# Token-major x and its logits: one 144-column product per 128 features, or a transposition and a 16-column product, on one Trainium2 core

## The chip, the core and the metric

The kernel runs on one core of a Trainium2 chip. The metric is device time in microseconds of one execution. Five engines work at the same time and wait for one another through semaphores: TensorE (PE, with its weight loads listed apart as PEld), VectorE (DVE), ScalarE (ACT), GpSimd (POOL) and SyncE (SP), which here only issues transfers. TensorE reads SBUF and writes PSUM; DVE and ACT take its results from there. A product on TensorE has two operands: one is loaded into the array first (lhsT, the weights), the other streams through it (rhs).

## What is computed

A retention layer feeds a mixture of experts that uses one expert for each token:

```python
scores = (q @ k.T) / 8 * Dmat            # 8 batches, 8 heads, 576 positions, 64 wide; Dmat[i,j] = gamma_h**(i-j) for i >= j
x = (scores @ v), as 4608 tokens x 512   # heads side by side
logits = x @ w_gate                      # 512 x 8
e = argmax(logits); gate = softmax(logits)[e]
eom = sigmoid(x @ w_output_gate)         # 512 x 8
out[token] = gate * eom[e] * relu(x @ w1[e]) @ w2[e]     # w1: 512 x 1024, w2: 1024 x 512, 8 experts
```

## The kernel before

The 4608 tokens are 36 tiles of 128. The work has two parts.

The first part is a loop over the tiles, `for g in range(NTILE)`, whose order is written out by hand under `tc.manual_schedule()`. In iteration g TensorE does, in this order: the scores of tile g+1 (`scores`, L361), the share of the running state in the output of tile g (`by_state`, L403), the share of the scores (`outT`, L412), the new state (`update`, L388), every fourth time a handful of small bf16 products for the slots of four tiles (`gate2`, L453 to L464), then k of tile g+1 turned to tokens (`k_rows`, L342) for some tiles, and last `xnat(g-1)` (L525). The state is reset every nine tiles (CPB), so `update` and `by_state` do nothing there. ACT copies state, k and x out of PSUM (L390, L344, L529) and casts expert weights; DVE masks the scores (L372), scales x (L416), and does the gate; POOL scales v (`prep`, L348) and scatters rows of x to a buffer in DRAM, sorted by expert (L191), with a small memset ahead of each scatter as a spacer.

`xnat` is what the change is about. `outT` leaves x of a tile as `xT`, 4 blocks of 128 features by 128 tokens. The experts want rows of x by tokens, and the gate wants 16 numbers a token (8 logits, 8 output gates). Both come from one product per block: lhsT is the block, rhs is `iw`, a constant of 144 columns that holds the identity (128 columns) and the 16 gate columns of that block side by side. In fp32 each product is two records in the trace, so a tile has 8 records, 4 into the bank `xa` and 4 into the bank `xb`. The gate columns lie so that in each bank the 16 columns of two blocks fall on the same place and add up. ACT then copies the tokens of each bank (two copies of 128x256), and DVE copies the 16 columns of `xa` and adds those of `xb` (L534, L535).

The state update needs k by tokens. It is loaded as features by tokens (in `pack`), and turned in one of two ways: by four transpositions against the identity on TensorE, 128x128 each and one record each, with a copy of 128x512 on ACT (`k_rows`); or by a second transfer of 256 KB from `krow`, a copy of k in DRAM by tokens (`load_k`). `by_rows(g)` says which: by transfer for odd g from 3 to 31. Tiles with g % 9 == 8 need none.

The second part, from 161 us on, is the experts: for each, h = x w1 and y = h w2 in products of fp32r with a high and a low part (L258, L279), weights streamed in by SP and split by ACT and DVE (L140, L145). Slots that got no token are filled by POOL scatters, with `G.memset(iw, 0.0)` ahead of each as a spacer (L709).

Of the kernel before, what the change touches and what calls it, by code (L numbers as in the profile page):

```python
# [10 lines left out]
F32 = mybir.dt.float32  # L11
# [4 lines left out]
ALU = mybir.AluOpType  # L16
# [7 lines left out]
DM = H * D  # L24
E = 8
F = 1024
P = 128
NP = H // 2
# [6 lines left out]
SNAP = 5  # L35
# [5 lines left out]
GT = 4  # L41
# [7 lines left out]
def tile_retention_moe(  # L49
# [17 lines left out]
    V, A, G, T, SP = nc.vector, nc.scalar, nc.gpsimd, nc.tensor, nc.sync  # L67

    const = ctx.enter_context(tc.tile_pool(name="const", bufs=1))
# [14 lines left out]
    ident = cmat_sb[:, 0, 0, :]  # L84
    gq_sb = const.tile([P, NP, 640], F32, name="gq_sb")
    gk_sb = const.tile([P, CPB, H, 1], F32, name="gk_sb")
    iw = const.tile([P, NP, 144], F32, name="iw")
    cbf_sb = const.tile([P, 2, P], BF16, name="cbf_sb")
    csm_sb = const.tile([P, 16 + 2 * CT], F32, name="csm_sb")
    base2 = const.tile([P, 1, E], F32, name="base2")  # L90
# [6 lines left out]
    xgrp = [const.tile([P, GT, XW], F32, name=f"xgrp{i}") for i in range(2)]  # L97
# [8 lines left out]
    def load_rest(step):  # L106
        if step < 3:
            n = slice(P * (step + 2), P * (step + 3))
            SP.dma_start(out=gq_sb[:, :, n], in_=gq[:, :, n])
        if step == 0:  # L110
            for p in range(NP):
                o = 0 if p % 2 == 0 else 16
                V.tensor_copy(iw[:, p, o:o + P], ident)
        elif step == 1:
            SP.dma_start(out=cmat_sb[:, 3], in_=cmat[:, 3])
        elif step == 2:
            SP.dma_start(out=cbf_sb, in_=cbf)
            SP.dma_start(out=csm_sb, in_=csm)
            SP.dma_start(out=tok_sb, in_=tokid)
            SP.dma_start(out=cov_sb, in_=cov)  # L120
            for x in xgrp:
                G.memset(x[:, :, DM:XW], 0.0)
            G.memset(zx.bitcast(I32)[:, DM:DM + 1], NT)
# [169 lines left out]
    ps_1 = p1ctx.enter_context(tc.tile_pool(name="ps_1", bufs=1, space=PSUM))  # L293
    ps_s = psctx.enter_context(tc.tile_pool(name="ps_s", bufs=1, space=PSUM, side="right"))

    pk, kn, vs, xT, gt = {}, {}, {}, {}, {}
# [10 lines left out]
    def load_first():  # L307
        t = [ld.tile([P, 3, 512], F32, name="pk") for _ in range(4)]
        pk.update(enumerate(t))
        SP.dma_start(out=t[0][:, 1], in_=pack[0, :, 1])  # L310
        A.dma_start(out=t[0][:, 0], in_=pack[0, :, 0])
        SP.dma_start(out=cmat_sb[:, 0:3], in_=cmat[:, 0:3])
        A.dma_start(out=t[0][:, 2], in_=pack[0, :, 2])
        SP.dma_start(out=gk_sb, in_=gk)
        A.dma_start(out=t[1][:, 0:2], in_=pack[1, :, 0:2])
        SP.dma_start(out=gq_sb[:, :, 0:P], in_=gq[:, :, 0:P])
        SP.dma_start(out=t[1][:, 2], in_=pack[1, :, 2])
        wgv = wg.rearrange("(p c) g -> c p g", c=P)
        SP.dma_start(out=iw[:, 0:NP:2, P:144], in_=wgv[:, 0:NP:2])
        SP.dma_start(out=iw[:, 1:NP:2, 0:16], in_=wgv[:, 1:NP:2])  # L320
        for i in (2, 3):
            if i == 3:
                SP.dma_start(out=gq_sb[:, :, P:2 * P], in_=gq[:, :, P:2 * P])
            SP.dma_start(out=t[i][:, 0:2], in_=pack[i, :, 0:2])
            SP.dma_start(out=t[i][:, 2], in_=pack[i, :, 2])

    def by_rows(g):
        return g % 2 == 1 and 1 < g < GT * SNAP + 12

    def load_k(g):  # L330

        if g < NTILE and g % CPB != 8 and by_rows(g):
            kn[g] = wk.tile([P, DM], F32, name="kn")
            SP.dma_start(out=kn[g], in_=krow[g])

    def k_rows(g):

        if g % CPB == 8 or by_rows(g):
            return
        ps = ps_s.tile([P, NP, P], F32, name="k_ps")  # L340
        for p in range(NP):
            T.transpose(ps[:, p, :], pk[g][:, 1, P * p:P * p + P], ident)  # L342
        kn[g] = wk.tile([P, DM], F32, name="kn")
        A.copy(out=kn[g], in_=ps.rearrange("p a i -> p (a i)"))  # L344
# [76 lines left out]
    def gate1a(n):  # L421
        L = gt["lg"]
        l, z = L[:, :, 0:8], L[:, :, 8:16]
        bc = lambda a: a.broadcast_to([P, GT, E])
        mx = sm.tile([P, GT, 1], F32, name="mx")
        V.tensor_reduce(out=mx, in_=l, op=ALU.max, axis=AX.X)
        lm = sm.tile([P, GT, E], F32, name="lm")
        V.tensor_tensor(out=lm, in0=l, in1=bc(mx), op=ALU.subtract)
        fst = sm.tile([P, GT, E], F32, name="fst")
        V.tensor_tensor(out=fst, in0=l, in1=bc(mx), op=ALU.is_equal)  # L430
        gt["half"] = (n, fst, lm, z)
# [85 lines left out]
            V.tensor_tensor(out=base2[:, 0, 0:1], in0=base2[:, 0, 0:1], in1=bump, op=ALU.add)  # L517

    def xnat(g):
        xa = ps_1.tile([P, 512], F32, name="xa")  # L520
        xb = ps_1.tile([P, 512], F32, name="xb")
        for p in range(NP):
            dst = xa if p < 2 else xb
            o = 0 if p % 2 == 0 else P
            i = T.matmul(dst[:, o:o + 144], lhsT=xT[g][:, p, :], rhs=iw[:, p, :],  # L525
                         start=(p % 2 == 0), stop=(p % 2 == 1), skip_group_check=True)
        x = xgrp[g // GT % 2][:, g % GT]
        for i, b in enumerate((xa, xb)):
            A.copy(out=x[:, 2 * P * i:2 * P * i + 2 * P].rearrange("p (a c) -> p a c", a=2),  # L529
                   in_=b[:, 0:288].rearrange("p (a c) -> p a c", a=2)[:, :, 0:P])  # L530
        if g % GT == 0:
            gt["lg"] = sm.tile([P, GT, 16], F32, name="lg")
        L = gt["lg"][:, g % GT]
        V.tensor_copy(L, xa[:, P:144])  # L534
        V.tensor_tensor(out=L, in0=xb[:, P:144], in1=L, op=ALU.add)  # L535

    load_first()
    V.memset(zx, 0.0)

# [24 lines left out]
    with tc.manual_schedule():  # L564
        k_rows(0)
        S_next = scores(0)
        for g in range(NTILE):
            S_sb = S_next
            prev = stcur[0] if g % CPB != 0 else None
            if g < 4:  # L570
                load_rest(g)
# [37 lines left out]
            if g > 0:  # L609
                xnat(g - 1)  # L610
# [21 lines left out]
    mm1(0, 0, 0)  # L632
    mm1(0, 0, 1)
    xnat(NTILE - 1)
    gate1a(NTILE // GT - 1)
    gate1b()
# [69 lines left out]

    def fill_slots(e):
        for f in fills[e]:
            G.memset(iw, 0.0)  # L709
            f()  # L710

    mctx.enter_context(tc.manual_schedule())
# [2 lines left out]
    load_idx(0, 1)  # L715
    w = [start_w(1, 1, fp) for fp in range(2)]
    fill_slots(1)
    fill_slots(0)
    for fb in range(5, FB):
        mm1(0, 0, fb)  # L720
# [9 lines left out]
    for e in range(E):  # L730
        nx = e + 1 < E
        for fb in range(FB):
            if e > 0:
                mm1(e, 0, fb)
            mm1(e, 1, fb)
            if e > 0 and fb < 4:
                load_w(2, e, fb)
            if e == 0:

                if fb in (0, 2):  # L740
                    w.append(start_w(1, 1, 2 + fb // 2))
                if fb in (1, 3, 5):
                    load_x(1, 2 + fb // 2)
                if fb % 2 == 1:
                    hi_w(*w[fb // 2])
                    lo_w(*w[fb // 2])
            elif nx:
                if fb < CT:
                    load_x(e + 1, fb)
                if fb in (5, 6):  # L750
                    load_idx(e + 1, fb - 5)
                if fb in (5, 7):
                    load_w(1, e + 1, (fb - 5) // 2)
            if fb == (7 if e else 4) and e + 2 < E:
                fill_slots(e + 2)
# [19 lines left out]
    with ExitStack() as octx:  # L775
# [3 lines left out]
        with tc.For_i(0, n, 1) as i:  # L779
            e = nc.values_load(ovt[0:1, 0, bass.ds(i, 1)], engines=[mybir.EngineType.SP], min_val=0, max_val=E - 1)  # L780
            o = nc.values_load(ovt[0:1, 1, bass.ds(i, 1)], engines=[mybir.EngineType.SP], min_val=0,
                               max_val=E * NT - P)
            x = ov.tile([P, XW], F32, name="ox")
            SP.dma_start(out=x, in_=xs[bass.ds(o, P), :])
            wa = ov.tile([P, KB, F], F32, name="wa")
            for fp in range(4):
                SP.dma_start(out=wa[:, :, 256 * fp:256 * fp + 256],
                             in_=w1[bass.ds(e, 1), fp].rearrange("a p (k f) -> p (a k) f", k=KB))
            wb = ov.tile([P, FB, DM], F32, name="wb")
            for fp in range(4):  # L790
                SP.dma_start(out=wb[:, 2 * fp:2 * fp + 2],
                             in_=w2[bass.ds(e, 1), fp].rearrange("a p (k c) -> p (a k) c", k=2))
# [6 lines left out]
            for fb in range(FB):  # L799
                h_ps = ps_v.tile([P, P], F32, name="oh_ps")  # L800
                for k in range(KB):
                    T.matmul(h_ps, lhsT=wa[:, k, P * fb:P * fb + P], rhs=oxT[:, k, :],
                             start=(k == 0), stop=(k == KB - 1))
                A.activation(out=oh[:, fb], in_=h_ps, func=AF.Relu)
            y_ps = ps_v.tile([P, DM], F32, name="oy_ps")
            for fb in range(FB):
# [4 lines left out]
                                 in_=y, in_offset=None, bounds_check=NT - 1, oob_is_err=False)  # L811
# [71 lines left out]
```

## Time and profile before

| | |
|---|---|
| median of 3 runs | 611.01 us (610.93 to 611.16) |
| profiled execution, its own time | 610.17 us |
| its span, first to last instruction | 608.3 us |
| mean granted TensorE clock | 0.999 |
| first part (tiles), until the first product of the experts | 161.35 us of the span |
| second part (experts) | from there to the end |

The profile gives for each engine how long it was busy, for each group of instructions its count, busy time and mean duration, and the idle time just ahead of it with what ended it. In the timeline a row is a run of like instructions: its start, how long until the last of them ended, and how many. A product on TensorE is pipelined: the duration of one record reaches well past the start of the next, so what a record costs is read from the distance of starts, and a busy TensorE can still hide small holes.

### The profile page before, as it was taken

How to read it: one execution, taken by the hardware profiler on the slowest of the kernel's cores; microseconds unless marked ns; L12 is line 12 of the kernel's file. 1: busy time of each engine (PE TensorE's matmuls, PEld its weight loads, DVE VectorE, ACT ScalarE, POOL GpSimd, SP SyncE). 2: the span in 40 equal slices, each digit the busy share in tenths (PEclk: the TensorE clock that was granted, in tenths of full speed). 3: DMA queues.
4: the chain of work that ended last, by engine and by line, in shares of the span. 5: the costliest groups of instructions: out<-in, count | busy, mean ns of one | idle time of the engine just before them, and what ended most of it. 6: DMA issues, size and time to landing. Idle time of an engine off the chain costs nothing. (4 is left out here: it accounts for less than half of the span.)

```text
span 608.3 us, 13984 instructions
## 1 busy us (share of the span) xinstructions
PE 594.3 (98%) x5688; PEld 528.6 (87%) x5688; DVE 331.1 (54%) x735; ACT 218.9 (36%) x477; POOL 187.1 (31%) x235
## 2 busy tenths in 40 slices
PE   8999999999999999999999999999999999999995
PEld 5889898878898999879978987997899799889974
DVE  4589888888650765625543563445265435626410
ACT  2334333333321544325332533443354234325110
POOL 2245544475456623016013301601240110110011
PEclk9999999999999999999999999999999999999999
DMA  9989888985226676435243634434363435221011
GB/s 310 358 302 327 318 309 323 345 272 192 86 97 194 163 204 179 149 104 161 85 135 116 174 106 140 116 131 139 97 190 88 123 104 147 92 84 52 1 38 41
DMA packets 56925, 100.28 MB, mean 165 GB/s; under 512 B 14967, under 2 KB 35832, under 8 KB 56860
## 3 DMA queue, kind: packets, MB, share of 16 engines
q1 hardware_dynamic: 46988, 76.72, 40.5%
q0 software_dynamic: 9440, 21.60, 9.7%
q8 instruction: 45, 0.74, 0.5%
q10 hardware_dynamic: 432, 1.05, 0.4%
q14 instruction: 20, 0.16, 0.1%
HBM read 77.75 MB, written 31.18 MB: 179 GB/s over the span
## 5 line engine op out<-in xcount | busy, mean ns | idle before, releaser
L258 PE MATMUL h_ps<-xh,w1h 128*128 128x360 f32 (+1 forms) x512 | 155.0, 303 | 0.1
L258 PE MATMUL h_ps<-xh,w1l 128*128 128x360 f32 (+1 forms) x512 | 154.8, 302 | 0.0
L258 PE MATMUL h_ps<-xl,w1h 128*128 128x360 f32 (+1 forms) x512 | 154.7, 302 | 0.0
L285 POOL DMA_INDIRECT out_dram<-y,idx x40 | 39.7, 993 | 317.0 <-ACT y L284 271.8
L266 DVE SCALAR_TENSOR_TENSOR hl<-h_ps,hh 128x360 fp32r<-128x360 f32 (+1 forms) x128 | 61.2, 478 | 129.6 <-ACT hh L265 117.9
L279 PE MATMUL y_ps<-w2h,hh 128*128 128x512 f32 (+1 forms) x320 | 126.1, 394 | 0.0
L279 PE MATMUL y_ps<-w2l,hh 128*128 128x512 f32 (+1 forms) x320 | 125.9, 394 | 0.0
L279 PE MATMUL y_ps<-w2h,hl 128*128 128x512 f32 (+1 forms) x320 | 125.1, 391 | 0.0
L265 ACT ACTIVATE hh<-h_ps 128x360 fp32r<-128x360 f32 (+1 forms) x128 | 54.8, 428 | 117.9 <-PE h_ps L258 112.4
L258 PEld LDWEIGHTS h_ps<-xh,w1h 128*128 128x128 f32 x512 | 96.0, 187 | 0.7 <-DVE xl L242 0.3
L258 PEld LDWEIGHTS h_ps<-xl,w1h 128*128 128x128 f32 x512 | 95.9, 187 | 0.3
L258 PEld LDWEIGHTS h_ps<-xh,w1l 128*128 128x128 f32 x512 | 96.1, 188 | 0.0
L284 ACT ACTIVATE y<-y_ps,idx 128x512 f32<-128x512 f32 (+1 forms) x40 | 27.5, 688 | 141.4 <-issue 91.5
L279 PEld LDWEIGHTS y_ps<-w2h,hl 128*128 128x128 f32 (+1 forms) x320 | 58.8, 184 | 15.3
L279 PEld LDWEIGHTS y_ps<-w2h,hh 128*128 128x128 f32 (+1 forms) x320 | 58.8, 184 | 14.8
L145 DVE TENSOR_TENSOR w1l<-st,w1h 128x512 fp32r<-128x512 f32 x64 | 44.9, 737 | 49.2 <-ACT w1h L140 47.8
L279 PEld LDWEIGHTS y_ps<-w2l,hh 128*128 128x128 f32 (+1 forms) x320 | 58.8, 184 | 14.0
L191 POOL DMA_INDIRECT xs<-xgrp,sli x36 | 38.7, 1074 | 61.8 <-issue 20.5
L191 POOL DMA_INDIRECT xs<-zx,fill x42 | 45.4, 1081 | 7.2 <-issue 6.8
L372 DVE TENSOR_TENSOR S_sb<-sc,cmat_sb 128x512 f32<-128x512 f32 x64 | 41.0, 682 | 11.0 <-PE sc L361 10.5
L348 POOL TENSOR_TENSOR vp<-pk,gk_sb 128x512 f32<-128x512 f32 x36 | 37.7, 1049 | 29.9 <-PE st_ps L388 14.0
L145 DVE TENSOR_TENSOR w2l<-st,w2h 128x512 fp32r<-128x512 f32 x64 | 44.6, 735 | 2.3
(128 smaller groups left out, 671.9 us busy)
## 6 DMA issues: line engine op xcount, KB each, us to landing
st<-in_w_dram SPq DMA_DIRECT2D x64, 512.0 KB
pk<-in_pack_dram SPq DMA_DIRECT2D x32, 768.0 KB
x_q<-xs SPq DMA_DIRECT2D x140, 64.0 KB
kn<-in_krow_dram SPq DMA_DIRECT2D x14, 256.0 KB
gq_sb<-in_gq_dram SPq DMA_DIRECT2D x5, 256.0 KB
pk<-in_pack_dram SPq DMA_DIRECT2D x4, 256.0 KB
pk<-in_pack_dram SPq DMA_DIRECT2D x2, 512.0 KB
x_g<-xs SPq DMA_DIRECT2D x4, 256.0 KB
```

The source lines that it names most:

```text
L145: V.tensor_tensor(out=lo[:, k], in0=st[:, k], in1=hi[:, k].bitcast(F32), op=ALU.subtract)
L191: i = G.indirect_dma_start(out=xs, out_offset=bass.IndirectOffsetOnAxis(ap=at, axis=0), in_=x, in_offset=None, **({} if bound is None else ...
L258: i = T.matmul(ps, lhsT=a[:, k, :], rhs=b[:, k, 0:n], start=(j == 0), stop=(j == 3 * KB - 1))
L265: A.activation(out=hh, in_=ps, func=AF.Relu)
L266: V.scalar_tensor_tensor(out=hl, in0=ps, scalar=0.0, in1=hh.bitcast(F32), op0=ALU.max, op1=ALU.subtract)
L279: i = T.matmul(ps, lhsT=a[:, n], rhs=b, start=(j == 0), stop=(j == 3 * FB - 1))
L284: A.activation(out=y, in_=ps, func=AF.Copy, scale=idx.bitcast(F32)[0:m, e, t, 1:2])
L285: G.indirect_dma_start(out=out, out_offset=bass.IndirectOffsetOnAxis(ap=idx[0:m, e, t, 0:1], axis=0), in_=y, in_offset=None, bounds_check= ...
L348: G.tensor_tensor(out=vs[g], in0=pk[g][:, 2].rearrange("p (h d) -> p h d", h=H), in1=gk_sb[:, g % CPB].broadcast_to([P, H, D]), op=ALU.mult)
L372: V.tensor_tensor(out=v(S_sb[:, r].rearrange("p a i -> p (a i)")), in0=v(sc[:, r]), in1=cmat_sb[:, 1:3].rearrange("p c a i -> p a (c i)"). ...
```

## The change

`xnat` makes x by tokens with four transpositions of 128x128 against the identity (the form that `k_rows` has), all into the one bank `xa`, and the 16 gate numbers with four fp32 products of 16 columns that add up in a bank of their own, `xl`. The blocks of `xT` are loaded as weights for the transpositions and once more for the products. ACT copies one 128x512 instead of two 128x256, DVE copies 128x16 once and adds nothing. `iw` is gone: the gate columns are loaded as `wg_sb` by one transfer instead of two, DVE's four copies of the identity into `iw` at the start are gone, and POOL's spacer in the experts' part clears a tile of its own, `pad`. `by_rows` also takes the even tiles 30 and 32, so two tiles' four transpositions of k and their ACT copies become two transfers of 256 KB.

```diff
-        if step == 0:
-            for p in range(NP):
-                o = 0 if p % 2 == 0 else 16
-                V.tensor_copy(iw[:, p, o:o + P], ident)
-        elif step == 1:
+        if step == 1:
...
     def by_rows(g):
-        return g % 2 == 1 and 1 < g < GT * SNAP + 12
+        return g > 1 and (g % 2 == 1 or g > GT * SNAP + 9) and g < GT * SNAP + 13
...
     def xnat(g):
-        xa = ps_1.tile([P, 512], F32, name="xa")
-        xb = ps_1.tile([P, 512], F32, name="xb")
+        xa = ps_1.tile([P, NP, P], F32, name="xa")
+        xl = ps_1.tile([P, 512], F32, name="xl")
         for p in range(NP):
-            dst = xa if p < 2 else xb
-            o = 0 if p % 2 == 0 else P
-            i = T.matmul(dst[:, o:o + 144], lhsT=xT[g][:, p, :], rhs=iw[:, p, :],
-                         start=(p % 2 == 0), stop=(p % 2 == 1), skip_group_check=True)
-        x = xgrp[g // GT % 2][:, g % GT]
-        for i, b in enumerate((xa, xb)):
-            A.copy(out=x[:, 2 * P * i:2 * P * i + 2 * P].rearrange("p (a c) -> p a c", a=2),
-                   in_=b[:, 0:288].rearrange("p (a c) -> p a c", a=2)[:, :, 0:P])
+            T.transpose(xa[:, p], xT[g][:, p, :], ident)
+        for p in range(NP):
+            T.matmul(xl[:, 0:16], lhsT=xT[g][:, p, :], rhs=wg_sb[:, p, :], start=p == 0, stop=p == NP - 1)
+        A.copy(out=xgrp[g // GT % 2][:, g % GT, 0:DM], in_=xa.rearrange("p a c -> p (a c)"))
...
-        L = gt["lg"][:, g % GT]
-        V.tensor_copy(L, xa[:, P:144])
-        V.tensor_tensor(out=L, in0=xb[:, P:144], in1=L, op=ALU.add)
+        V.tensor_copy(gt["lg"][:, g % GT], xl[:, 0:16])
```

On TensorE, in iteration 29 before (k of tile 30 is turned at L342, then x of tile 28), the order is:

```order
L412 MATMUL o_ps<-S_sb,vp 64x128 x8
L388 MATMUL st_ps<-vp,kn 64x64 x8
L342 MATMUL k_ps<-cmat_sb,pk 128x128 x4
L525 MATMUL xa<-iw,xT 128x144 x2
L525 MATMUL xb<-iw,xT 128x144 x2
L361 MATMUL sc<-pk 64x64 x16
```

In the same iteration of the changed kernel, whose line numbers are 5 or more lower, it is:

```order
L407 MATMUL o_ps<-S_sb,vp 64x128 x8
L383 MATMUL st_ps<-vp,kn 64x64 x8
L518 MATMUL xa<-cmat_sb,xT 128x128 x4
L520 MATMUL xl<-wg_sb,xT 128x16 x4
L356 MATMUL sc<-pk 64x64 x16
```

The four transpositions of k are gone here, and the four products of 144 columns are four transpositions (against `cmat_sb`, which holds the identity) and four products of 16 columns. In the other tiles the k row stays where it stood, and only the x rows differ so.

On SP, the queue of transfers, the last of the loop before stand so (kn is k by tokens, pk the packed tile):

```order
L334 DMA kn<-in_krow_dram 128x512
L304 DMA pk<-in_pack_dram 128x1536 x2
L334 DMA kn<-in_krow_dram 128x512
L304 DMA pk<-in_pack_dram 128x1536 x2
L159 DMA x_g<-xs 128x512 x2
```

and now:

```order
L329 DMA kn<-in_krow_dram 128x512
L301 DMA pk<-in_pack_dram 128x1536
L329 DMA kn<-in_krow_dram 128x512
L301 DMA pk<-in_pack_dram 128x1536
L329 DMA kn<-in_krow_dram 128x512
L301 DMA pk<-in_pack_dram 128x1536
L329 DMA kn<-in_krow_dram 128x512
L301 DMA pk<-in_pack_dram 128x1536
L156 DMA x_g<-xs 128x512 x2
```

Two transfers of k came in between those of the last tiles, ahead of the first reads of sorted rows.

More of the change, by code (lines that the diff above doesn't have):

```diff
@@ L86, in tile_retention_moe @@
     gk_sb = const.tile([P, CPB, H, 1], F32, name="gk_sb")
-    iw = const.tile([P, NP, 144], F32, name="iw")
+    wg_sb = const.tile([P, NP, 16], F32, name="wg_sb")
+    pad = const.tile([P, 512], F32, name="pad")
     cbf_sb = const.tile([P, 2, P], BF16, name="cbf_sb")
@@ L317, in load_first @@
         SP.dma_start(out=t[1][:, 2], in_=pack[1, :, 2])
-        wgv = wg.rearrange("(p c) g -> c p g", c=P)
-        SP.dma_start(out=iw[:, 0:NP:2, P:144], in_=wgv[:, 0:NP:2])
-        SP.dma_start(out=iw[:, 1:NP:2, 0:16], in_=wgv[:, 1:NP:2])
+        SP.dma_start(out=wg_sb, in_=wg.rearrange("(p c) g -> c p g", c=P))
         for i in (2, 3):
@@ L708, in fill_slots @@
         for f in fills[e]:
-            G.memset(iw, 0.0)
+            G.memset(pad, 0.0)
             f()
```

## The prediction

> **What bounds the kernel now.** I read the page first: how busy each engine is, and in which slices of the span.
>
> ```profile
> PE 594.3 (98%) x5688; PEld 528.6 (87%) x5688; DVE 331.1 (54%) x735; ACT 218.9 (36%) x477; POOL 187.1 (31%) x235
> PE   8999999999999999999999999999999999999995
> DMA  9989888985226676435243634434363435221011
> ```
>
> TensorE works in every slice; no other engine is near. The transfers are heavy in the first nine slices, which are the tiles, where all that the change touches lies. So the busy time by stretch comes next, then what TensorE waited for.
>
> ```profile
> 20.00:120.00 100.00, 98.72 (x2137) 87.92 (x2138) 82.83 (x239) 36.22 (x104) 47.19 (x65) 1.00 0.91 324
> 120.00:161.00 41.00, 38.53 (x757) 33.88 (x749) 35.19 (x110) 14.94 (x41) 21.70 (x33) 1.00 0.57 193
> ```
>
> ```profile
> PE sc L541 <- DVE zx L538: 1.5, 1, 1.5
> PE o_ps L403 <- issue: 1.2, 4, 0.3
> PE o_ps L412 <- DVE S_sb L372: 0.9, 1, 0.9
> PE k_ps L232 <- PE xb L525: 0.5, 1, 0.5
> ```
>
> The first column after the span is TensorE: 98.72 of 100 us, then 38.53 of 41. The four longest waits of TensorE stand here, 4.1 us together; none is on a transfer, and the transfers, at a share of 0.91, keep up. A record's duration covers small holes, so I checked with the timeline how a tile goes, by distances of starts:
>
> ```profile
> 93.01 0.63 PE L388 MATMUL st_ps<-vp,kn 128*64 128x64 f32 x16
> 93.57 0.76 PE L525 MATMUL xa<-iw,xT 128*128 128x144 f32 x4
> 94.17 0.65 PE L525 MATMUL xb<-iw,xT 128*128 128x144 f32 x4
> 94.75 0.69 PE L361 MATMUL sc<-pk 64*64 64x64 f32 x32
> 95.26 0.62 PE L403 MATMUL o_ps<-pk,stT 64*64 64x128 f32 x16
> 95.81 1.09 PE L412 MATMUL o_ps<-S_sb,vp 128*64 128x128 f32 x16
> 96.74 0.64 PE L388 MATMUL st_ps<-vp,kn 128*64 128x64 f32 x16
> 97.30 0.66 PE L342 MATMUL k_ps<-cmat_sb,pk 128*128 128x128 f32 x4
> 97.80 0.66 PE L525 MATMUL xa<-iw,xT 128*128 128x144 f32 x4
> 98.29 0.65 PE L525 MATMUL xb<-iw,xT 128*128 128x144 f32 x4
> 98.88 0.90 PE L361 MATMUL sc<-pk 64*64 64x128 f32 x32
> ```
>
> Each group begins where the one before it lets go. The tile from 94.75 to 98.88 takes 4.13 us: 0.51 scores, 0.55 state, 0.93 output, 0.56 update, 0.50 k, 1.08 x. TensorE's own issue is the bound, so what the change adds to its row of work is added to the time.
>
> **What x costs now.** Behind k, x takes 98.88 - 97.80 = 1.08 us; behind the update, whose shape differs (64 columns of weights), 94.75 - 93.57 = 1.18, since its first load of weights is then not hidden. Inside, four records take 98.29 - 97.80 = 0.49, 0.1225 each. The last four take 0.59: three distances of 0.1225 and 0.22 from the last start to the next group's. k's four transpositions take 97.80 - 97.30 = 0.50 behind the update. Hidden behind others they would take less, because the first of them, too, shows its load.
>
> **What the new pieces cost.** The transposition is the row of k: same form, same identity. The 16-column product is in no row, so I split it into its streaming and its load of weights, by the groups of like shapes:
>
> ```profile
> L412 PE MATMUL o_ps<-S_sb,vp 128*64 128x128 f32 x576 | 40.3, 279 | 2.2 <-DVE S_sb L372 0.9 <-issue 0.6 <-POOL gap L622 0.6
> L388 PE MATMUL st_ps<-vp,kn 128*64 128x64 f32 x448 | 18.5, 223 | 0.5 <-issue 0.4
> L525 PEld LDWEIGHTS xb<-iw,xT 128*128 128x128 f32 x144 | 20.1, 190 | 0.0
> L388 PEld LDWEIGHTS st_ps<-vp,kn 128*64 128x64 f32 x448 | 17.0, 138 | 1.0 <-issue 0.8
> L342 PEld LDWEIGHTS k_ps<-cmat_sb,pk 128*128 128x128 f32 x72 | 7.7, 143 | 2.9 <-issue 1.9
> ```
>
> Streaming 64 fp32 columns more (128 against 64) lengthens a record by 279 - 223 = 56 ns: 0.87 ns a column, about 14 ns for 16. Loading 64 columns more of fp32 weights lengthens a load by 190 - 138 = 52 ns, 0.81 a column, 104 ns for 128 columns. A load in a transposition is 47 ns shorter (143). So in the old record the load (104) hides behind 144 streaming columns (0.1225 us a record); in the new one it can't hide behind 14 ns, and the load is the pace. The nearest row of a pace near the load is the experts' products of 256 columns, with the same 128x128 weights, twelve of them from the first row to the second:
>
> ```profile
> 231.12 0.28 PE L258 MATMUL h_ps<-xh,w1h 128*128 128x256 f32 x1
> 232.49 0.32 PE L258 MATMUL h_ps<-xh,w1h 128*128 128x360 f32 x1
> ```
>
> 1.37 us for 12 is 114 ns. A pace below 104 would have the load run faster than its rows show; above 122 there is no reason for. I take 113 ns, the row it is nearest to, and keep 104 and 122 as the ends. A product stays two records, as in xa (x144 for 36 tiles and two products), so a tile has 8 of them.
>
> The Trainium skill, "TensorE: Matmul & The Clock Gate", section "Back-to-back issue gap", says that in a stream of loads and products the spacing is set by both, and the section on LDWEIGHTS gives 1/1.2 ns a column of weights, whatever the contraction. By that figure a load of 128 columns is an estimated 107 ns, and the sum below would be about 1.5 us smaller; it speaks against the change as the rows do.
>
> **The sum for a tile.** Behind the update: four transpositions up to the next start, 0.50 as for k; 7 distances of 0.113 = 0.79; from the last start to the next group's, the old 0.22 less the streaming saved (0.12 - 0.014), 0.11. Together 1.40 against 1.18: **+0.22**. Behind k the first transposition's load is hidden: four distances near the 0.107 that 128 columns stream (0.1225 x 128/144 = 0.109), 0.44, so 1.34 against 1.08: **+0.26**. In the two tiles without k: before 0.50 + 1.08 = 1.58, now 1.40: **-0.18**.
>
> k's row counts x72, 18 tiles; 16 of them are followed by x (tiles 0 and 1 are not). Two lose it: 14 x 0.26 = 3.6, 2 x -0.18 = -0.4, and 20 tiles without k x 0.22 = 4.4. Sum **+7.7 us**. With 104 ns it is 36 x 7 x 0.009 = 2.3 less, +5.4; with 122, 2.3 more, +10.0.
>
> **What lies beside.** ACT and DVE save work:
>
> ```profile
> L529 ACT COPY xgrp<-xb 128x256 f32<-128x256 f32 x36 | 13.7, 380 | 2.3 <-PE xb L525 0.4
> L344 ACT COPY kn<-k_ps 128x512 f32<-128x512 f32 x18 | 10.6, 587 | 7.9 <-PE k_ps L342 7.3 <-PE xa L525 0.4
> L535 DVE TENSOR_TENSOR lg<-xb,lg 128x16 f32<-128x16 f32 x36 | 6.3, 175 | 5.1 <-ACT xgrp L529 1.8 <-DVE lg L534 0.3
> ```
>
> One copy of 512 columns (587 ns, as kn's) for two of some 376: 36 x 0.165 = 5.9 us less on ACT, and 2 x 0.587 for k; 36 x 0.175 = 6.3 us less on DVE. TensorE waits for neither in the steady tile, so I count nothing; if it did somewhere, the gain there is at most the 0.9 + 0.5 us of its listed waits on DVE. I count -0.5: at the handover to the experts TensorE stands 0.5 us ahead of L232 for the PSUM tile that DVE is still reading, and a longer x there eats that wait. The two k transfers go past the pk of tiles 34 and 35 in SP's queue, 0.5 MB, about 1.6 us at 324 GB/s; they are issued when the state update two tiles earlier frees the buffer, some 8 us ahead of their use (two tiles of 4.1), in a stretch with a DMA share of 0.57, so nothing waits. If one came late, the tile would stand for about 1 us. The four identity copies at the start lie in a stretch where TensorE waits for the first transfers, the POOL spacers are off the path: nothing for either.
>
> So +7.7 - 0.5 = +7.2. On the profiled execution, 608.3 us of span in 610.17 of time, that is 617.4. The median of the runs stands 0.84 above that execution, and on it, 611.01, the forecast is **618.2 us**.
>
> **Rivals.** *The loads are not the pace (faster).* The small bf16 products of the gate follow each other closely:
>
> ```profile
> 136.52 0.22 PE L458 MATMUL k_ps<-oh,cbf_sb 128*128 128x24 bf16 x3
> 136.60 0.74 PE L525 MATMUL xa<-iw,xT 128*128 128x144 f32 x4
> ```
>
> Three in 0.08 us, about 25 ns each, on 128x128 weights. If a 16-column fp32 product went so, 36 x 7 x (0.113 - 0.025) = 22 us less: 618.2 - 22 = 596 us. The sign turns at a pace of 0.113 - 7.2/252 = 0.084 us. Against it: those weights are bf16, and the fp32 load's slope of 0.81 ns a column is in 448 records. 8%. The same section of the Trainium skill gives 25 ns as the floor for 1 to 64 columns, and 81 ns for a stream of 128-column products with their loads; at 81 the forecast would be an estimated 0.9 us under the old time. No fp32 row here shows either.
>
> *The added work falls into holes (little or no change).* TensorE does stop in seven tiles, in the middle of a group. The first, one between and the last of these rows:
>
> ```profile
> 22.61 0.44 PE L412 MATMUL o_ps<-S_sb,vp 128*64 128x128 f32 x4 [0.59 <-issue]
> ...
> 74.25 0.80 PE L403 MATMUL o_ps<-pk,stT 64*64 64x128 f32 x14
> 75.35 0.38 PE L403 MATMUL o_ps<-pk,stT 64*64 64x128 f32 x2 [0.29 <-issue]
> 75.65 0.55 PE L412 MATMUL o_ps<-S_sb,vp 128*64 128x128 f32 x6
> ...
> 143.44 0.51 PE L403 MATMUL o_ps<-pk,stT 64*64 64x128 f32 x9 [0.30 <-issue]
> ```
>
> The state group at 74.25 takes 75.65 - 74.25 = (to the next group's start at 75.65) 1.40 us instead of 0.55, 0.85 too much. If all seven ended at a time that something else sets, each could swallow what x added just before, 7 x 0.26 = 1.8 us: 616.4. If, with fewer DVE and ACT instructions, the holes went altogether, 7 x 0.85 = 6.0 us: 612.2, no change that could be told. The releaser is "issue", nothing the change touches. 10%.
>
> *Slower still.* If products that add up on the same 16 columns, or the second load of the same block, went at 0.1225 or the 24 records for 16 a tile (loads and products) thinned TensorE's issue: +10.0 or more, 621 and above. 9%.
>
> *The change doesn't do what it says*, a transposition in two records: 36 x 4 x 0.11 = 16 us more, 634. k's x72 for 18 tiles speaks against it. 1%.
>
> **How the numbers follow.** My forecast with paces of 104 to 122 ns, 615.7 to 620.7, has 72%. The range goes down to 614.0, into the second rival, and up to 621.5, into the third, and leaves out the first, the fourth and the tails. Under 0.2% (1.2 us), about the least that a measurement can tell from no change, would lie between 609.8 and 612.2: 4%. Faster 9%: the first rival, and a little of holes that go in full. Slower 87%.
>
> **What would show it.** In the changed kernel's timeline x should take 1.40 us behind the update, 1.34 behind k, its four transposition records 0.109 apart, its eight 16-column records 0.10 to 0.12 apart with loads of about 190 ns. The first product of the experts starts so before:
>
> ```profile
> 161.35 0.43 PE L258 MATMUL h_ps<-xh,w1h 128*128 128x360 f32 x1
> ```
>
> It should start near 161.35 + 7.2 = 168.5 us, and from there the two kernels run alike. A pace under 0.084, or a start before 161, would make the forecast wrong in sign; a start at 168 with another total would mean the experts' part moved.

## The result, and the profile after

| | before | changed |
|---|---|---|
| median of 6 runs | 610.97 us (610.61 to 613.51) | 616.91 us (616.32 to 621.02) |
| profiled execution, its own time | 610.17 us | 616.32 us |
| its span | 608.3 us | 614.5 us |
| first product of the experts | 161.35 us | 167.24 us |

The ratio is 1.0106, 95% interval 1.0081 to 1.0131: slower by 5.9 us, where 7.2 was forecast. The page of the changed kernel, engines and transfers, first:

```profile
PE 601.5 (98%) x5824; PEld 540.0 (88%) x5824; DVE 324.1 (53%) x695; ACT 214.3 (35%) x439; POOL 183.7 (30%) x235
DMA  9988888886315667343442724444263335321001
```

TensorE has 5824 records for 5688: 36 tiles have 12 in x instead of 8 (+144), and two tiles lost 4 of k (-8). DVE and ACT have less to do (324.1 us for 331.1, 214.3 for 218.9); what that is worth is a question of the third set of runs. The timeline of TensorE, a tile with k turned on TensorE, then the x of one without:

```profile
75.57 0.63 PE L383 MATMUL st_ps<-vp,kn 128*64 128x64 f32 x16
76.13 0.66 PE L337 MATMUL k_ps<-cmat_sb,pk 128*128 128x128 f32 x4
76.63 0.60 PE L518 MATMUL xa<-cmat_sb,xT 128*128 128x128 f32 x4
77.06 0.96 PE L520 MATMUL xl<-wg_sb,xT 128*128 128x16 f32 x8
77.96 0.90 PE L356 MATMUL sc<-pk 64*64 64x128 f32 x32
80.16 0.63 PE L383 MATMUL st_ps<-vp,kn 128*64 128x64 f32 x16
80.72 0.66 PE L518 MATMUL xa<-cmat_sb,xT 128*128 128x128 f32 x4
81.22 0.96 PE L520 MATMUL xl<-wg_sb,xT 128*128 128x16 f32 x8
82.11 0.33 PE L356 MATMUL sc<-pk 64*64 64x128 f32 x4
```

Behind k, x takes 77.96 - 76.63 = 1.33 us (forecast 1.34, before 1.08); behind the update 82.11 - 80.72 = 1.39 (forecast 1.40, before 1.18). By form, the new records and the copies that follow them:

```profile
L520 PEld LDWEIGHTS xl<-wg_sb,xT 128*128 128x128 f32 x288 | 35.0, 192 | 0.0
L518 PEld LDWEIGHTS xa<-cmat_sb,xT 128*128 128x128 f32 x144 | 15.9, 141 | 1.1 <-issue 0.3
L521 ACT COPY xgrp<-xa 128x512 f32<-128x512 f32 x36 | 21.1, 586 | 10.0 <-PE xa L518 6.1 <-PE o_ps L407 3.1 <-PE xl L520 0.3
```

The 16-column products are 288 records (eight a tile), each with a load of 192 ns; the loads of a tile begin 0.112 us apart. The starts of the eight products stand 0.03 apart once and 0.112 apart six times, and 0.19 lie between the last of them and the next group, 0.90 in all from 77.06 to 77.96. The transpositions are 144 records. At the end of the tiles TensorE stood 0.52 us at L232 (now L229) in the kernel before. The profile names TensorE's own group there; DVE's last read of that bank (L474) ended at 157.18, just before the first load of L232 at 157.26:

```profile
157.04 0.14 DVE L474 COPY cnt<-k_ps 128x1 f32<-128x1 f32 x1
157.29 0.72 PE L232 MATMUL k_ps<-cmat_sb,x_g 128*128 128x128 f32 x4 [0.52 <-PE xb L525]
```

The same place in the changed kernel:

```profile
161.93 0.64 PE L518 MATMUL xa<-cmat_sb,xT 128*128 128x128 f32 x4
162.40 0.96 PE L520 MATMUL xl<-wg_sb,xT 128*128 128x16 f32 x8
163.21 0.70 PE L229 MATMUL k_ps<-cmat_sb,x_g 128*128 128x128 f32 x4
...
167.24 0.41 PE L255 MATMUL h_ps<-xh,w1h 128*128 128x360 f32 x1
```

L229 follows x with no wait. The experts begin 167.24 - 161.35 = 5.89 us later. From there the changed kernel takes 447.26 us and the one before 446.95, 0.31 less; the x of the last tile stands in this part. So nearly all of the change lies in the tiles.

The account, by median distances of starts, of the 35 x that stand ahead of the experts' first product: behind k 14 x 0.254, behind the update or the gate's products 17 x 0.208, two behind the output together 0.19, two tiles without k 2 x -0.185, together +6.9 us (forecast +7.7 for all 36). The wait at the handover took 0.5 of it, as forecast. The holes in the middle of groups, each against the median of its kind of group and summed over the tiles, are 6.0 us before and 5.2 after, 0.8 less. 6.9 - 0.5 - 0.8 = 5.6, against 5.89 measured. Summed from start to start without medians, the rows of x take 7.00 us more (the handover's wait is taken off in it), those of k 1.04 less, and all others together 0.07 less.

### The profile page after: what moved, and what is told of

Read it like the earlier page. It is cut to its first block, busy times and chain, and to the rows that moved or that the text cites. A ratio compares the mean times of both kernels' runs of the same rounds, so it can differ in the third digit from the quotient of the medians.

```text
span 614.5 us, 14156 instructions
## 1 busy us (share of the span) xinstructions
PE 601.5 (98%) x5824; PEld 540.0 (88%) x5824; DVE 324.1 (53%) x695; ACT 214.3 (35%) x439; POOL 183.7 (30%) x235
## 5 line engine op out<-in xcount | busy, mean ns | idle before, releaser
L188 POOL DMA_INDIRECT xs<-zx,fill x42 | 44.0, 1047 | 7.1 <-issue 7.1
```

The source lines that it names most:

```text
L188: i = G.indirect_dma_start(out=xs, out_offset=bass.IndirectOffsetOnAxis(ap=at, axis=0), in_=x, in_offset=None, **({} if bound is None else ...
```

## The experiments

The theory was that of the prediction: TensorE's issue is the bound, loads of weights are the pace of the short products, and a record more or less shows in the time. The rivals: the streaming is the pace; the holes give way to added work, or something outside TensorE sets the end of the tiles; and, once the chips differed, the copies that the change took from ACT and DVE. The letters are those of the expectations. The runs came in three sets, each on a chip of its own, with the kernel before run among them: 609.73 us on the first chip (25 runs), 611.57 on the second (23), 610.12 on the third (24). Of the kernel before there is one profile, that of the result's section; on these chips it was timed only.

### First set

**The two transfers of k alone.** The kernel before, with

```diff
-        return g % 2 == 1 and 1 < g < GT * SNAP + 12
+        return g > 1 and (g % 2 == 1 or g > GT * SNAP + 9) and g < GT * SNAP + 13
```

> The kernel before with the change to by_rows alone: k of tiles 30 and 32 by transfer, x as before. Theory A (TensorE's own issue is the bound, the transfers have room): each of the two tiles loses four transpositions, 0.49 us by the distances in the trace, so about 1.0 us less than before, 610.0 against 611.0. Rival C (the two transfers come late, or push the last packed tiles back): no gain, or up to 1 us more than before, and a state update of tile 30 or 32 that waits for a DMA.

Measured 610.06 us (12 runs), ratio 1.0009 (0.9992 to 1.0026): no gain. By distances of starts a tile without k's turn saves 0.493 + 1.076 - 1.178 = 0.39 us, since x then stands behind the update; where an expectation counts k's whole 0.49, it is 0.10 too much. The 0.8 us of two tiles, too, lies outside the interval, which ends at -0.5. TensorE waits for no transfer of k. It stops for "issue", and once, 1.75 us, for POOL. One stop for "issue", the stretch it lies in, and the wait for POOL:

```profile
98.65 0.33 PE L403 MATMUL o_ps<-pk,stT 64*64 64x64 f32 x9
99.74 0.34 PE L403 MATMUL o_ps<-pk,stT 64*64 64x64 f32 x7 [0.76 <-issue]
```

```profile
20.00:120.00 100.00, 98.48 (x2143) 87.86 (x2141) 85.85 (x241) 37.95 (x104) 48.48 (x65) 1.00 0.92 324
```

```profile
141.61 1.44 POOL L191 DMA_INDIRECT xs<-xgrp,sli  x1 [0.22 <-ACT xgrp L529]
143.07 1.05 POOL L348 TENSOR_TENSOR vp<-pk,gk_sb 128x512 f32<-128x512 f32 x1
144.17 1.09 PE L412 MATMUL o_ps<-S_sb,vp 128*64 128x128 f32 x16 [1.75 <-POOL gap L622]
```

The holes of this kernel add up to 6.6 us, this wait among them.

**The new x alone.** The changed kernel with the old `by_rows`, the diff above the other way round.

> The changed kernel with the old by_rows: x by transpositions and 16-column products, k as before. Theory A: 16 tiles behind k at +0.25 and 20 others at +0.21 us are +8.2 us, less the 1.4 us that fewer or shorter holes gave back in the changed kernel, so about +6.9: 617.9, and 1.0 above the changed kernel. Rival C: the same as the changed kernel or below it.

Measured 612.76 us (7 runs), ratio 1.0051 (1.0032 to 1.0069). x takes as long as in the changed kernel, yet the time rises by 3.0 us only. The holes are down to 1.8 us. So on this chip the added work does fall into holes: 6.6 - 1.8 = 4.8 us of it, if the kernel with k's transfers stands for the one before. 1.8 of them are the wait for POOL, which the new x alone doesn't have.

**Transpositions and products in turn.** The product follows the transposition of the same block:

```diff
         for p in range(NP):
             T.transpose(xa[:, p], xT[g][:, p, :], ident)
-        for p in range(NP):
             T.matmul(xl[:, 0:16], lhsT=xT[g][:, p, :], rhs=wg_sb[:, p, :], start=p == 0, stop=p == NP - 1)
```

> The changed kernel with the same instructions in another order: the product of a block stands right behind its transposition (T P T P T P T P instead of TTTT PPPP). Theory A (eight loads of 0.112 us one behind the other are the pace, and a load hides only behind streaming): the first load of each product hides behind the 0.109 us that the transposition streams, so a block takes 0.109 + 0.112 + 0.056 = 0.277 us; x behind k 1.16 instead of 1.33, behind the update 1.22 instead of 1.39, 36 x 0.17 = 6.1 us less than the changed kernel: about 611. Rival B (what costs is the number of records, or eight records that add up on the same 16 columns): order doesn't matter, or more changes of form cost more: 616.9 or above.

The timeline of x behind k:

```profile
74.16 0.66 PE L337 MATMUL k_ps<-cmat_sb,pk 128*128 128x128 f32 x4
74.65 0.27 PE L518 MATMUL xa<-cmat_sb,xT 128*128 128x128 f32 x1
74.76 0.29 PE L519 MATMUL xl<-wg_sb,xT 128*128 128x16 f32 x2
74.90 0.31 PE L518 MATMUL xa<-cmat_sb,xT 128*128 128x128 f32 x1
...
75.84 0.90 PE L356 MATMUL sc<-pk 64*64 64x128 f32 x32
```

x takes 75.84 - 74.65 = 1.19 us, 1.25 behind the update. The theory of loads as the pace holds: a load behind a transposition lies under its 128 streaming columns, and only the loads behind 16 columns show; the count of records is the same. The whole came to 610.10 us (12 runs), ratio 1.0007 (0.9990 to 1.0025), with holes of 3.1 us.

**96 columns for 16.** The product's rhs is padded with zeros to 96 columns; the first 16 results are the same.

```diff
-            T.matmul(xl[:, 0:16], lhsT=xT[g][:, p, :], rhs=wg_sb[:, p, :], start=p == 0, stop=p == NP - 1)
+            T.matmul(xl[:, 0:96], lhsT=xT[g][:, p, :], rhs=wg_sb[:, p, 0:96], start=p == 0, stop=p == NP - 1)
```

> The changed kernel with products of 96 columns instead of 16, the other 80 columns zero and never read; the spacer in the experts' part clears the widened tile. Theory A: 96 columns stream in about 0.083 us, less than a load, so the records stay 0.112 us apart and only the last one of a tile lets go 0.067 us later: 36 x 0.067 = 2.4 us more than the changed kernel, 619.3. Rival D (streaming is the pace): each of eight records grows by 0.067 us, 36 x 8 x 0.067 = 19 us more, 636.

```profile
76.34 0.60 PE L518 MATMUL xa<-cmat_sb,xT 128*128 128x128 f32 x4
76.78 1.03 PE L520 MATMUL xl<-wg_sb,xT 128*128 128x96 f32 x8
77.74 0.90 PE L356 MATMUL sc<-pk 64*64 64x128 f32 x32
```

x takes 1.40 us for 1.33: six times the columns cost 0.066 us a tile. The loads stay 0.112 us apart; only the next group's first load comes later, 0.286 behind the last of them for 0.219. Streaming is not the pace, the loads are. The time was 613.78 us (5 runs), ratio 1.0078 (1.0051 to 1.0104).

### Second set

**The changed kernel again**, unchanged, beside what follows.

> The changed kernel itself, beside the others on one chip. Theory F (TensorE's holes are late blocks of its own instructions: in the traces they stand 256 records, or a multiple of that, apart; how many there are varies from run to run and chip to chip, and a longer x gives the blocks more time): the trace shows x at 1.33 behind k and 1.39 behind the update again, +7.4 us in all, and the difference from before is 7.4 less what the holes give back, which is anything from 1 to 5 us: 2.5 to 6.5 us. Theory A alone (the added issue is the whole of it): 7 us again.

Measured 616.67 us (6 runs), ratio 1.0087 (1.0068 to 1.0106), holes of 5.2 us in the same tiles as in the result's profile.

**The new x with the old copies.** The new x alone, with ACT and DVE given back what the change saved them:

```diff
-        A.copy(out=xgrp[g // GT % 2][:, g % GT, 0:DM], in_=xa.rearrange("p a c -> p (a c)"))
+        x = xgrp[g // GT % 2][:, g % GT]
+        for i in range(2):
+            A.copy(out=x[:, 2 * P * i:2 * P * i + 2 * P].rearrange("p (a c) -> p a c", a=2), in_=xa[:, 2 * i:2 * i + 2])
...
-        V.tensor_copy(gt["lg"][:, g % GT], xl[:, 0:16])
+        for _ in range(2):
+            V.tensor_copy(gt["lg"][:, g % GT], xl[:, 0:16])
```

> As x only, but with the work that the change saved on ACT and DVE put back: two copies of 256 columns and two copies of the 16 logits a tile (the second writes the same numbers again). Theory F: the holes don't ask how busy ACT and DVE are, so the time is that of x only, 3.0 us above before, within 1. Rival G (the holes are TensorE waiting on ACT and DVE in a way that the profile doesn't name, and went because these had less to do): holes come back to some 6 to 7 us in the trace, and the time is 5 to 8 us above before.

Measured 618.52 us (5 runs), ratio 1.0116 (1.0098 to 1.0133), holes of 5.6 us: 6.9 us slower than before, where the new x alone on the first chip cost 3.0. Either the copies matter or the chip does; the third set was for that.

**Five more tiles of k by transfer** (22, 24, 28, 30 and 32; the expectation leaves out 28, but TensorE has 5668 records for 5688, 20 fewer), and **all 14 that were left from tile 2 to 32**, in the kernel before:

```diff
-        return g % 2 == 1 and 1 < g < GT * SNAP + 12
+        return g > 1 and (g % 2 == 1 or g > GT * SNAP + 1) and g < GT * SNAP + 13
```

```diff
-        return g % 2 == 1 and 1 < g < GT * SNAP + 12
+        return 1 < g < GT * SNAP + 13
```

> The kernel before with k by transfer for the even tiles 22, 24, 30 and 32 as well, x as before. Theory A: 4 x 0.49 = 2.0 us less than before. Theory F: two of the four lie where the transfers' share is 0.9, so the gain there goes into holes, as in the run with two tiles; 0 to 1 us less than before.

> The kernel before with k by transfer for every tile from 2 to 32, 14 more than before, 3.7 MB more in some 140 us. Theory A: 14 x 0.49 = 6.9 us less than before. Theory F: the transfers' share goes from 0.91 to nearly 1 and TensorE asks for its instructions sooner, so holes grow; from 3 us less to 3 us more than before.

Measured 611.03 us (10 runs, 0.9989, 0.9976 to 1.0001) and 611.39 us (12 runs, 0.9998, 0.9984 to 1.0012). Five tiles take 5 x 0.39 = 2.0 us of work away, and the first interval ends at -1.5. With all 14, 14 x 0.39 = 5.5 us of TensorE's work is taken away and the time stays. The stretch of the tiles, and one stop:

```profile
20.00:120.00 100.00, 96.16 (x2107) 85.32 (x2099) 84.47 (x236) 31.93 (x92) 48.88 (x65) 1.00 0.95 345
```

```profile
60.61 0.65 PE L412 MATMUL o_ps<-S_sb,vp 128*64 128x128 f32 x8 [0.97 <-issue]
```

TensorE is 96.16 of 100 us busy for 98.72 before, the transfers' share is 0.95 for 0.91, and the holes come to 10.1 us, for the 6.0 of the result's profile of before: most of what the work gave up, the stops took. The theory falls here: TensorE's own work is not the bound alone.

### Third set

> The x-only kernel once more, now on the same chip as the next three. Theory F, sharpened by the traces (how many holes TensorE has differs by chip, not by the copies): within 1 us of the kernel with the old copies, and about 1.0 us above the changed kernel, which has two tiles' transpositions of k less. Rival G (fewer copies, fewer holes): 3 to 4 us below the kernel with the old copies.

> The x-only kernel with the old number of copies on ACT and DVE, on the same chip as x-only. Theory F: the same as x-only within 1 us. Rival G: 3 to 4 us above x-only, and holes of 5 to 6 us in its trace where x-only has under 2.

> The changed kernel on the same chip. Theory F: about 1.0 us below x-only. Rival G: the same as x-only or above it, as in the first two comparisons on different chips (5.1 to 5.9 above before, against 3.0).

> The alternating order on the same chip as the changed kernel. By the trace of its first run x takes 1.19 behind k and 1.25 behind the update, 0.14 less than in the changed kernel: theory A says 36 x 0.14 = 5.0 us below the changed kernel, less what holes take up. Rival B (order doesn't matter): the same as the changed kernel.

The edits are those above.

| kernel | median (runs) | ratio to before | first product of the experts | holes |
|---|---|---|---|---|
| new x alone | 612.40 us (9) | 1.0040 (1.0021 to 1.0059) | 163.25 us | 1.8 us |
| new x, old copies | 613.54 us (7) | 1.0058 (1.0036 to 1.0080) | 164.51 us | 3.3 us |
| the changed kernel | 612.37 us (9) | 1.0040 (1.0024 to 1.0056) | 163.14 us | 2.6 us |
| in turn | 609.46 us (12) | 0.9987 (0.9972 to 1.0003) | 161.20 us | 3.4 us |

The copies are worth about 1 us at most, not 4. The changed kernel and the new x alone are equal, so the two transfers of k gave nothing here either. And the changed kernel, the same program, is 2.3 us slower than before on this chip, where it was 5.1 on the second and 5.9 in the result. How much of the added 7 us shows differs from set to set, and so by the chip, or by something else that differs between the sets. In turn, x costs 0.14 us a tile less, 5 us in 36 tiles, and 2.9 us of it show. No version is clearly faster than the kernel before.

### Three sorts of stops

The traces of these runs show three sorts of holes on TensorE. One is the plain wait for POOL above: in the last tiles POOL has two scatters a tile, and v for TensorE's output (L348) stands behind them. It is 0.56 us in the kernel before, 1.75 in that with k's transfers alone, 1.37 with all of k by transfer, and none in the changed kernel of the result. The other two go by the name of "issue".

**Every 256 instructions.** In the kernel in turn (first chip) the stops stand at fixed distances in TensorE's program, whatever the tile is doing. The first row is one of them. Below it stand stretches from one stop's end to the next one's; behind the length of the stretch come TensorE's busy time with its products, and the same for its loads of weights (x128 is 128 of them), then DVE, ACT and POOL, the clock, the transfers' share and GB/s:

```profile
134.63 0.18 PE L519 MATMUL xl<-wg_sb,xT 128*128 128x16 f32 x1 [1.23 <-issue]
```

```profile
22.50:29.21 6.71, 6.26 (x128) 5.59 (x128) 3.16 (x6) 1.92 (x4) 1.73 (x2) 1.00 0.95 375
...
98.27:115.99 17.72, 17.26 (x380) 15.88 (x380) 14.92 (x38) 6.26 (x14) 8.80 (x12) 1.00 0.83 284
115.99:134.63 18.64, 17.41 (x380) 16.27 (x380) 17.34 (x49) 5.81 (x14) 10.52 (x16) 1.00 0.87 312
134.63:140.92 6.29, 5.66 (x127) 5.12 (x127) 5.91 (x20) 2.48 (x6) 2.30 (x5) 1.00 0.87 299
```

128 products and 128 loads are 256 instructions; 380 and 380, with the 7 or 8 semaphore instructions that the view doesn't count, 767 and 768, three times 256. Counted so, each of these stops comes at instruction 193 or 194 past a multiple of 256; so do six stops of the kernel with k's transfers alone, and five in the kernel with all of k by transfer. The page of the changed kernel has a queue for instructions:

```profile
q8 instruction: 46, 0.75, 0.5%
```

46 packets of 16 KB for 11,648 products and loads are 253 a packet. So TensorE's program itself comes by transfer in blocks, beside everything else. The times of these packets show that TensorE stops where the next block isn't there yet. The 14 traces have 331 places of this sort (194 past a multiple of 256) between 20 and 165 us. None is passed sooner than 1.25 us after its packet landed. 58 are passed within 1.56 us of the landing, and among them are all 32 stops of 0.4 us or more (by distances of starts); at the 273 whose packet landed earlier there is none of even 0.25 us. The Trainium skill, "Runtime: NRT & Kernel Launch", section "Instruction fetch mechanics", has blocks of 16 KiB and 256 instructions, which agrees, and the crossing "mostly hidden": at transfer shares of 0.83 to 0.95 it cost here up to 1.2 us a stop.

**While POOL scatters.** The third sort comes at no such distance. The first below is the changed kernel in the result's run, the second the same kernel on the third chip, both at the same place of the program (rows of TensorE, POOL and DVE):

```profile
63.89 0.90 PE L356 MATMUL sc<-pk 64*64 64x128 f32 x32
64.53 1.01 POOL L188 DMA_INDIRECT xs<-xgrp,sli  x1 [0.15 <-issue]
64.95 0.62 PE L407 MATMUL o_ps<-S_sb,vp 128*64 128x128 f32 x4
65.86 0.88 PE L407 MATMUL o_ps<-S_sb,vp 128*64 128x128 f32 x12 [0.29 <-issue]
65.97 1.29 DVE L367 TENSOR_TENSOR S_sb<-sc,cmat_sb 128x512 f32<-128x512 f32 x2 [1.21 <-PE sc L356]
```

```profile
63.44 0.90 PE L356 MATMUL sc<-pk 64*64 64x128 f32 x32
63.85 1.25 POOL L188 DMA_INDIRECT xs<-xgrp,sli  x1 [0.17 <-issue]
64.50 1.09 PE L407 MATMUL o_ps<-S_sb,vp 128*64 128x128 f32 x16
64.77 1.28 DVE L367 TENSOR_TENSOR S_sb<-sc,cmat_sb 128x512 f32<-128x512 f32 x2
```

In the first, TensorE starts nothing from about 65.3 to 65.86, which is 1.33 us past the scatter's start, and DVE, which waits for the scores begun at 63.89, starts 2.08 us later, at 65.97; in the second there is no hole, and DVE starts 1.33 us after the scores began. The trace's semaphore events (the signals by which engines release one another) tell it without the holes. Of the signals by which TensorE reports finished groups, those that came from 0.8 to 1.3 us after the start of a scatter, and from 1.3 to 1.6 us, over the 29 to 31 scatters between 10 and 152 us:

```
                                0.8-1.3   1.3-1.6
before, the result's profile        3        40
changed, the result's profile       0        36
second chip: changed                0        37
             x, old copies          0        35
             five tiles of k        2        32
             all of k               2        28
first chip:  k's transfers alone   23        13
             new x alone           22        15
             in turn               18        14
             96 columns            22        18
third chip:  new x alone           22        14
             x, old copies         25        14
             changed               22        18
             in turn               18        15
```

In the result's profiles and on the second chip TensorE's reports stand for half a microsecond in nearly every scatter and come together after it; on the other two chips they come about evenly. It isn't TensorE's alone: from 0.8 to 1.3 us DVE gives 7 signals and ACT 2 in the changed kernel of the result, 24 and 7 in the same kernel on the third chip. The same programs (changed; new x with old copies) are on both sides, so it doesn't go by the program; it goes by the chip, or by something else that differs between the sets. Why is open, and that TensorE's stop of some 0.55 us is a wait for one of these late signals is likely, not shown.

The sorts together give a reading of why one program costs 2.3 to 5.9 us; it is argued, not shown. Where the scatters hold TensorE, they do so before and after alike, TensorE rarely gets ahead of its program's blocks (one late block before and one after, both at 22.6 us), and added work adds: holes 6.0 us before, 5.2 after. Where they don't, the kernel before, if that with k's transfers stands for it, runs ahead until it meets late blocks and waits for POOL (3.7 us at six late blocks and 1.8 at POOL, of 6.6), and added work takes that place (1.8 to 2.6 us). The late blocks go with crowded transfers: in the 14 traces, from 20 to 162 us, the packet of a block starts 0.3 us (median of 37) after TensorE has passed the place before it where the transfers' share around that moment is under 0.6, and 2.7 us (median of 125) where it is 0.95 or more; the packet itself takes 1.0 us in both. That is a correlation: no run had the same program with fewer transfers. The scatters couldn't be taken out without other work for the experts, and that wasn't tried.

## Why the prediction was right, and where not

- **The price of the 16-column product** was right: 0.112 us a record for 0.113, set by the load of weights. That 96 columns cost 0.066 us a tile more and that taking turns saves 0.14, with the same records, shows it. The first rival (25 ns records) is out, and so are the 81 ns of the Trainium skill's page "TensorE: Matmul & The Clock Gate", section "Back-to-back issue gap", for these fp32 records.
- **x a tile** was right: +0.254 behind k for 0.26, +0.208 behind the update for 0.22, -0.185 for -0.18; +6.9 us over 35 tiles for +7.7 over 36. The split inside it was not: seven distances of 0.113 between the products and 0.11 behind the last start were forecast, and the starts show 0.03, six of 0.112 and 0.19. The stretch behind the last start hardly depends on the columns streamed (0.216 us with 144, 0.205 with 96, 0.193 with 16), where the prediction halved it. The two misses are 0.08 each and cancel, which is luck.
- **The handover's wait, -0.5**, was right: it is gone.
- **ACT's and DVE's savings** were counted at nothing. Giving the copies back cost about 1 us on the third chip; whether that is more than the noise of two medians (612.40 and 613.54, intervals of the ratios overlapping) is not settled.
- **"TensorE's own issue is the bound, so what the change adds to its row of work is added to the time"** is the step that failed in part. It held in the result's runs, 5.6 us by the account and 5.9 in the median, and about so on the second chip (5.1). It didn't on the first and third chip, where some 7 us of work (the changed kernel) and 8 us (the new x alone) came out as 2.3 to 3.0. It doesn't hold downwards at all: 0.8, 2.0 and 5.5 us of k's work taken off (2, 5 and 14 tiles) gave nothing that the intervals show. So it is in part luck of the chip that the time fell into the range: 2.3 us on top of the 611.01 that the forecast starts from would be 613.3, below the range's 614.0.
- **"The four longest waits of TensorE stand here"** was misread: two of 0.6 us were left out that are longer than the fourth, one for "issue" and one for POOL. Both belong to the stops that take up work given or taken:

```profile
PE o_ps L412 <- issue: 0.6, 1, 0.6
PE o_ps L412 <- POOL gap L622: 0.6, 1, 0.6
```

- **The two k transfers, -0.4 in the sum and "nothing waits"**: nothing waits for them, but they earn nothing either.
- **The second rival, "the added work falls into holes"**, was rejected because "issue" is nothing that the change touches. It touches it by being slower: a block that is late for a fast TensorE isn't for a slow one. It swallowed 0.8 us in the result's profile, within its 1.8, and some 4 to 5 us on two other chips, towards its 6.0.

## What to carry to other kernels

Price a short fp32 product by its load of weights, and put it behind a record that streams long enough to cover that load, not behind its own kind. Before a saving on a busy engine is counted, look at what its small "issue" stops have in common, their distance in instructions and the events of other engines at the same time: if something else sets them, work taken away only makes them longer. And where a change's cost rests on such holes, run it on more than one chip.

## What was not expected of the hardware

- TensorE's program comes in blocks of 256 instructions, and a late block stops TensorE for up to 1.2 us, with "issue" as the only name for it in the profile. No block was entered sooner than 1.25 us after its packet landed.
- On some chips the engines' reports of finished groups stand from 0.8 to 1.3 us after the start of nearly each POOL scatter (0 to 3 signals of TensorE for 18 to 25 on the others), and TensorE itself stops for about 0.55 us in several of them.
- So the same kernel stood at +5.9, +5.1 and +2.3 us to the kernel before, with intervals of 1.0081 to 1.0131, 1.0068 to 1.0106 and 1.0024 to 1.0056.
